# Loading the second half of an expert's weights one job later, behind the transpose of the next rows

## The chip, the core and the metric

The kernel runs on one core of one Trainium2 chip. The metric is the time of one execution on the device in microseconds (us); smaller is better. TensorE (PE in the profile), VectorE (DVE), ScalarE (ACT), GpSimd (POOL) and SyncE (SP) each work through a list of instructions of their own and wait for each other by semaphores. SP computes nothing here: it asks for transfers (DMAs), which 16 DMA engines carry out.

## What is computed

Two stages stand one behind the other. The first is a linear attention with a decaying state, over 4 batches, 8 heads, 768 steps and a head width of 48. Its output, 3072 tokens of 384 numbers, is routed: each token goes to the one expert of 8 with the largest logit.

```python
logits = x @ w_gate + modality_bias[modality_id]
e_idx = np.argmax(logits, axis=1)
...
for e in range(E):
    mask = e_idx == e
    if not mask.any():
        continue
    h = np.maximum(x[mask] @ w1[e], 0.0)          # 384 -> 1024
    out[mask] = gate_w[mask, None] * (h @ w2[e])  # 1024 -> 384
```

Only the experts' part is touched by the change. How many tokens an expert gets is known at run time alone.

## The kernel before

**Jobs.** The tokens of each expert lie side by side in `rows`, in device memory. A job is 128 rows of one expert: they are brought in transposed, multiplied by `w1`, passed through the relu, multiplied by `w2`, scaled and scattered to `out`. Each number is split into a high and a low half-precision part (`whi` and `wlo` for weights, `hh` and `hl` for the hidden layer), so each product is a few matmuls. The first jobs run beside the attention stage. The rest run in the loop at line 1660, whose bounds are read from a table at run time. An expert that is used has at least two jobs in the table; the ends of a run of jobs are marked there.

**One turn of the loop**, job `i`, in the order in which it is written: `finish_up` (the low part of the hidden layer of the job that was begun in the turn before), `take_in` (POOL copies the rows that have arrived, `xn`, to `mxT`, from which TensorE reads, and their gate weights and places, `mn`, to `m2`), `turn` (SP asks for the rows of the job after that: a transpose into `xn` and a small transfer into `mn`), then three branches on a code of the table. If the job is the first of an expert, `go_on` makes the rest of `whi` and `wlo` from the raw weights in `raw`, first `w1` and later, in `blocks(1, ...)`, `w2`. If the next job is the first of another expert, `by_both` takes the sums of squares of that expert's raw weights: ScalarE of the first half of `raw` (`w1`), VectorE of the second half (`w2`, tile `squares`). TensorE's small matmul `pw` (line 982) adds these sums up, and from it come the scales of the next expert's split. Between the branches stand TensorE's matmuls: `low_terms` (L1161), `raise_` (L1082), `high_terms` (L1156).

**The weights.** `raw` holds one expert in single precision, 128 partitions of 6144 numbers, 3 MB, of which `w1` is the first half and `w2` the second. There is one such buffer, so the next expert can be asked for only when the present one has been split. `next_load` does that near the end of the turn. It reads MORE from the table; if that isn't zero, SP issues two transfers of 1536 KB each (L965), one for each half:

```python
def next_load():
    more = self.at(MORE, i, 2 * E - 1, SP)
    with tc.If(more > 0):
        self.load(more % E, 2, 0, 1)
```

**Order.** Each engine runs its instructions in the order written; SP too, and SP's transfers go through one queue. A conditional whose body holds only SP's transfers appears on the other engines as one jump. Where a turn loads nothing, SP adds to the two semaphores that the loads would have added to, so that a wait can count turns; before it adds, it waits until the last load on that semaphore has landed. A reader of `raw` waits for the count that the last load ahead of it in the written order leaves.

Of the kernel before, what the change touches and what calls it, by code (L numbers as in the profile page):

```python
# [25 lines left out]
E = 8  # L26
# [38 lines left out]
ROW, CODE, MORE, SEEN = range(4)  # L65
SP, ACT, AD = (mybir.EngineType.SP,), (mybir.EngineType.Activation,), (mybir.EngineType.Activation, mybir.EngineType.DVE)
# [3 lines left out]
class _Kernel:  # L70
# [1148 lines left out]
    def run(self):  # L1219
# [20 lines left out]
        half = FB * HP // 2  # L1240
# [240 lines left out]
        i, j = NU - 2, NU - 1  # L1481
# [131 lines left out]
        def finish_up():  # L1613
            for g in (1, 2):
                self.relu_low(ph[g], *spans[g])
# [13 lines left out]
        def blocks(m, *at):  # L1629
            for lo, hi in zip(at, at[1:]):  # L1630
                self.broad(m, lo, hi)
                self.rest(m, lo, hi)

        def begin():
            self.broad(0, 0, F0 // 3)

        def go_on():
            self.rest(0, 0, F0 // 3)
            blocks(0, F0 // 3, F0, F0 + F0 // 2, WC)

        def by_both(cols):
            for q in range(NQ):
                if q < NQ // 2:
                    self.norm(junk, q)
                else:
                    part = self.raw[:, q * WQ : (q + 1) * WQ]
                    nc.vector.tensor_tensor_reduce(out=cols, in0=part, in1=part, scale=1.0, scalar=0.0, op0=ALU.mult, op1=ALU.add, accum_out=self.ssq[:, q : q + 1])

        def next_load():
            more = self.at(MORE, i, 2 * E - 1, SP)  # L1650
            with tc.If(more > 0):
                self.load(more % E, 2, 0, 1)

        self.wsb = self.late.tile([P, 1], F32, name="wsb")
        nc.vector.tensor_copy(self.wsb, self.ws[:, 1:])
# [4 lines left out]
        with tc.For_i(1, nj, 1, iteration_sync="reg_based") as i, tc.manual_schedule(engines={getattr(mybir.EngineType, e) for e in MS[:4]}):  # L1660
            finish_up()
            take_in(nc.gpsimd)
            self.turn(0, self.at(ROW, i, E * CAP, SP, 1), mn, xn)
            code = self.at(CODE, i, 15, AD)
            with tc.If(code % 8 > 3) as begun:
                go_on()
            with begun.Else():
                with tc.If(code % 2 > 0):
                    by_both(squares)
            self.low_terms(po)  # L1670
            self.put(po, 0, "b")
            with tc.If(code % 8 > 3):  # L1672
                self.undo()
                blocks(1, 0, F2 // 2, F2)
            self.due(m2, i)
            self.raise_(ph[0], *spans[0])
            self.relu_high(ph[0], *spans[0])
            self.raise_(ph[1], *spans[1])
            scaled = self.scales_("2")
            next(scaled)  # L1680
            with tc.If(code % 8 > 3) as first:
                blocks(1, F2, WC)
                self.relu_low(ph[0], *spans[0])
            with first.Else():
                self.relu_low(ph[0], *spans[0])
                for _ in scaled:
                    pass
                nc.vector.tensor_copy(self.wsb, self.ws[:, 1:])
            next_load()
            self.relu_high(ph[1], *spans[1])  # L1690
            self.raise_(ph[2], *spans[2])
            self.relu_high(ph[2], *spans[2])
            with tc.If(code > 7):
                begin()
            self.high_terms(po)
# [60 lines left out]
```

## Time and profile before

| what | value |
|---|---|
| median of 3 runs | 332.32 us (329.65 to 333.73) |
| the profiled execution's own time | 330.74 us |
| its span in the profile | 329.0 us |
| mean granted TensorE clock in it | 0.99 |
| TensorE busy with matmuls | 316.3 us, 96% of the span |
| turns of the loop that load weights | 1 (two transfers) |

The median is of executions without the profiler; the span is what the profiler saw, from first to last instruction, and the profiled execution's own time is 1.74 us more than that. TensorE's high share of busy time says that it seldom rests, not which of its rests the change can reach. For that the turns of the loop are read one by one.

### The profile page before, as it was taken

How to read it: one execution, taken by the hardware profiler on the slowest of the kernel's cores; microseconds unless marked ns; L12 is line 12 of the kernel's file. 1: busy time of each engine (PE TensorE's matmuls, PEld its weight loads, DVE VectorE, ACT ScalarE, POOL GpSimd, SP SyncE). 2: the span in 40 equal slices, each digit the busy share in tenths (PEclk: the TensorE clock that was granted, in tenths of full speed). 3: DMA queues.
4: the chain of work that ended last, by engine and by line, in shares of the span. 5: the costliest groups of instructions: out<-in, count | busy, mean ns of one | idle time of the engine just before them, and what ended most of it. 6: DMA issues, size and time to landing. Idle time of an engine off the chain costs nothing. (4 is left out here: it accounts for less than half of the span.)

```text
span 329.0 us, 13842 instructions
## 1 busy us (share of the span) xinstructions
PE 316.3 (96%) x5056; PEld 259.2 (79%) x5056; DVE 216.5 (66%) x705; ACT 159.4 (48%) x380; POOL 186.8 (57%) x298
## 2 busy tenths in 40 slices
PE   7999999989999999999999999999999999999983
PEld 3888888889797988879789688876688888887652
DVE  6987789795999899978768841276222223336780
ACT  4667677662367546657834341283222222226731
POOL 8997698954999897656377723234323322222212
PEclk9999999998999999999999999999999999999998
DMA  7869688959949954899978332119822212221100
GB/s 214 251 174 303 188 248 269 185 109 243 339 121 221 283 178 90 180 272 258 202 155 260 114 87 57 35 44 339 122 60 48 48 48 48 60 57 26 48 16 28
DMA packets 50748, 49.59 MB, mean 151 GB/s; under 512 B 35573, under 2 KB 44315, under 8 KB 50448
## 3 DMA queue, kind: packets, MB, share of 16 engines
q1 hardware_dynamic: 46480, 37.93, 48.5%
q0 software_dynamic: 3168, 9.47, 8.3%
q10 hardware_dynamic: 1056, 1.58, 1.4%
q8 instruction: 30, 0.49, 0.7%
q14 instruction: 14, 0.11, 0.1%
HBM read 30.55 MB, written 11.44 MB: 128 GB/s over the span
## 5 line engine op out<-in xcount | busy, mean ns | idle before, releaser
L1082 PEld LDWEIGHTS <-whi 128*128 128x128 f16 x1248 | 71.0, 99 | 4.8 <-issue 2.0
L1156 PEld LDWEIGHTS <-hh 128*128 128x128 f16 x384 | 36.1, 98 | 24.1 <-issue 1.8
L1082 PE MATMUL phb<-mxT,whi 128*128 128x128 f16 x672 | 44.5, 219 | 1.0 <-POOL mxT L1620 0.8
L1091 DVE SCALAR_TENSOR_TENSOR hl<-phb,hh 128x256 f16<-128x256 f32 (+1 forms) x42 | 20.1, 509 | 34.7 <-PE pw L982 17.9
L1082 PEld LDWEIGHTS <-wlo 128*128 128x128 f16 x624 | 37.0, 99 | 0.3 <-DVE wlo L1025 0.3
L380 POOL TENSOR_TENSOR rc<-ud,powr 112x512 f32<-112x512 f32 x23 | 30.4, 1323 | 9.3 <-DMA ud<-in_pd 9.2
L1086 ACT ACTIVATE hh<-phb 128x256 f16<-128x256 f32 (+1 forms) x42 | 18.8, 453 | 30.8 <-PE L1082 12.5
L682 POOL DMA_INDIRECT rows<-row,posi x24 | 26.1, 1089 | 10.7 <-issue 9.1
L1082 PE MATMUL phs<-mxT,whi 128*128 128x128 f16 x480 | 31.1, 223 | 0.9 <-DMA mxT<-rows 0.9
L458 DVE TENSOR_TENSOR at<-psc,mask 128x512 f32<-128x512 f32 x48 | 31.6, 680 | 0.1
L452 PE MATMUL psc<-rc,kc 64*128 64x128 f32 (+1 forms) x384 | 28.6, 285 | 0.8 <-DVE rc L380 0.4
L1161 PEld LDWEIGHTS <-hl 128*128 128x128 f16 x192 | 18.4, 98 | 13.6 <-issue 1.7
L564 ACT ACTIVATE row<-py,sx 128x384 f16<-128x384 f32 x24 | 13.9, 581 | 30.4 <-DVE sx L338 22.5
L452 PEld LDWEIGHTS psc<-rc,kc 64*128 64x128 f32 (+1 forms) x384 | 23.7, 187 | 3.8 <-issue 1.7
L1050 POOL TENSOR_TENSOR seenb<-otb,putb 128x1 int32<-128x1 int32 x13 | 3.8, 295 | 39.7 <-ACTq L1672 31.0
L487 PE MATMUL py<-kv,at 128*64 128x48 f32 x768 | 26.4, 222 | 0.0
L1156 PE MATMUL po<-wlo,hh 128*128 128x384 f16 x112 | 25.2, 326 | 1.1 <-DVE wlo L1025 1.1
L1082 PE MATMUL phb<-mxT,wlo 128*128 128x128 f16 x336 | 25.8, 219 | 0.2 <-DVE wlo L1025 0.2
L487 PEld LDWEIGHTS py<-kv,at 128*64 128x64 f32 x768 | 25.0, 138 | 0.5
L1620 POOL COPY mxT<-xn 128x768 f16<-128x768 f16 x13 | 10.8, 828 | 25.5 <-PE L1156 17.9
L1156 PE MATMUL po<-whi,hh 128*128 128x384 f16 x112 | 25.1, 326 | 0.0
L1039 ACT ACTIVATE otb<-po,fac 128x384 f32<-128x384 f32 x13 | 7.5, 577 | 34.8 <-PE phb L1082 31.6
(317 smaller groups left out, 690.5 us busy)
## 6 DMA issues: line engine op xcount, KB each, us to landing
ud<-in_pd SPq DMA_DIRECT2D x24, 384.0 KB, 4.9
kv<-in_pt SPq DMA_DIRECT2D x24, 384.0 KB, 4.6
raw<-in_w SPq DMA_DIRECT2D x12, 512.0 KB, 4.9
raw<-in_w SPq DMA_DIRECT2D x2, 1536.0 KB, 7.6
r<-in_pt SPq DMA_DIRECT2D x10, 192.0 KB, 6.2
rows<-pad ACTq DMA_DIRECT2D x1, 1544.0 KB, 6.8
rows<-row,posi POOLq DMA_INDIRECT x24, 5.0
xn<-rows SPq DMA_TRANSPOSE x14, 3.0
```

The costliest lines, as they stand in the source:

```text
L380: return (engine or nc.gpsimd).tensor_mul(u["rc"][:R, s], u["rT"][:, s], self.powr[:R, s])
L452: nc.tensor.matmul(u["ps"][j][:, pr * P : (pr + 1) * P], u["kc"][r, pr, :], u["rc"][r, pr, :], start=True, stop=True)
L458: return nc.vector.tensor_mul(u["at"][:, j * NPR : (j + 1) * NPR, :], u["ps"][j].rearrange("p (q t) -> p q t", q=NPR), self.mask.unsqueeze ...
L487: nc.tensor.matmul(py[t, sl], u["at"][:, j * NPR + pr, t], u["v"][:, sl], start=c == h == 0, stop=h == H - 1 and i >= BARE, skip_group_che ...
L564: self.nc.scalar.activation(u["x16"][:, :DM], u["x"], AF.Copy, scale=u["g"]["sx"][:, b : b + 1])
L682: i = nc.gpsimd.indirect_dma_start(out=self.rows, out_offset=bass.IndirectOffsetOnAxis(ap=u["posi"][:, b : b + 1], axis=0), in_=u["row"][: ...
L1082: self.nc.tensor.matmul(ph[:, q * n : (q + 1) * n], w[:, c0 : c0 + P], x[:, xq, :], start=i == q == 0, stop=i == len(terms) - 1, skip_grou ...
L1086: self.nc.scalar.activation(self.hh[:, f0 : f0 + fb, t * P : (t + 1) * P], p3, AF.Relu)
L1091: self.nc.vector.scalar_tensor_tensor(self.hl[:, f0 : f0 + fb, r], p3, 0.0, self.hh[:, f0 : f0 + fb, r], ALU.max, ALU.subtract)
L1156: self.nc.tensor.matmul(po[:, :DM], self.hh[:, f, t * P : (t + 1) * P], w[:, c0 : c0 + DM], start=n == 0, stop=False)
L1161: self.nc.tensor.matmul(po[:, :DM], self.hl[:, f, t * P : (t + 1) * P], self.whi[:, c0 : c0 + DM], start=False, stop=f == FB - 1)
L1620: take_in = lambda e: (e.tensor_copy(self.xT[:, :, :P], xn), e.tensor_copy(m2[:, 0, :], mn[:, 0, :]))
```

## The change

`next_load` gets two arguments: whose entry of the table is read, and which half is loaded. The first half (`w1`) is asked for where both were, near the end of turn `i`. The second half (`w2`) is asked for in turn `i + 1`, by the entry of job `i`, directly behind `turn`, which asks for the next rows. The table is now read twice in a turn by SP, and there are two conditionals in place of one.

```diff
-        def next_load():
-            more = self.at(MORE, i, 2 * E - 1, SP)
+        def next_load(job, half):
+            more = self.at(MORE, job, 2 * E - 1, SP)
             with tc.If(more > 0):
-                self.load(more % E, 2, 0, 1)
+                self.load(more % E, 2, half)
...
             self.turn(0, self.at(ROW, i, E * CAP, SP, 1), mn, xn)
+            next_load(i - 1, 1)
             code = self.at(CODE, i, 15, AD)
...
-            next_load()
+            next_load(i, 0)
             self.relu_high(ph[1], *spans[1])
```

On SP, before, the two halves (`raw`) stand one behind the other under one conditional, behind the transpose (`xn`) and the small transfer (`mn`); the words in brackets are the semaphores that each waits for, and DMAHW2 and DMAHW3 are those of the two loads:

```order
L1068 DMA_TRANSPOSE xn<-rows 128x6x128 [waits DMAHW0_I-4593_own,Pool_I-4593_own,DMAHW2_49]
L1665 UNCONDITIONAL_BRANCH
L1069 ISA
L1069 DMA mn<-rows 128x4 [waits DMAHW1_I-4593_own,Pool_I-4593_own,DMAHW3_49]
L1672 UNCONDITIONAL_BRANCH
L1681 UNCONDITIONAL_BRANCH
L951 ISA
L951 TENSOR_LOAD tab
L1651 COMPARE_AND_BRANCH
L965 ISA
L965 DMA raw<-in_w 128x3072 [waits DVE_I-4593_own,DMAHW2_I-4593_own,Activation_I-4593_own,Activation_49]
```

The next row but one there is the second half, on DMAHW3. After the change the load that comes first in the turn is the second half, and it now has DMAHW2; the first half comes after it, on DMAHW3:

```order
L1069 DMA mn<-rows 128x4 [waits DMAHW1_I-4593_own,Pool_I-4593_own,DMAHW3_49]
L951 ISA
L951 TENSOR_LOAD tab
L1651 COMPARE_AND_BRANCH
L965 ISA
L965 DMA raw<-in_w 128x3072 [waits DVE_I-4593_own,DMAHW2_I-4593_own,Activation_I-4593_own,Activation_49]
L1651 UNCONDITIONAL_BRANCH
L1651 UNCONDITIONAL_BRANCH [waits DMAHW2_I-4593_own]
L1666 UNCONDITIONAL_BRANCH
L951 ISA
L951 TENSOR_LOAD tab
L1651 COMPARE_AND_BRANCH
```

The second half has moved from behind the first half to the front of the following turn, behind `mn`. On VectorE, at the sums of squares of the next expert (`squares`, second half of `raw`), before:

```order
L951 TENSOR_LOAD tab
L1665 REGISTER_ALU
L1665 COMPARE_AND_BRANCH
...
L1668 COMPARE_AND_BRANCH
L1647 REGISTER_ALU
L1647 ISA squares,wssq<-raw 128x1024 [waits DMAHW3_I-4593_own,DVE_I-4593_own]
L1647 ISA wssq 128x1
```

And after:

```order
L1651 UNCONDITIONAL_BRANCH
L951 ISA
L951 TENSOR_LOAD tab
L1666 REGISTER_ALU
L1666 COMPARE_AND_BRANCH
...
L1669 COMPARE_AND_BRANCH
L1647 REGISTER_ALU
L1647 ISA squares,wssq<-raw 128x1024 [waits DMAHW2_I-4593_own,DVE_I-4593_own]
L1647 ISA wssq 128x1
```

VectorE waits for the semaphore of the second half as before. But the last load of it ahead of this instruction is now in the same turn, not in the one before, and there is a jump more (L1651) ahead of the table's read.

## Rows read from the trace of the kernel before

**Rows 1.** The page: span, busy time, and the loads issued inside the loop.

```profile
span 329.0 us, 13842 instructions
PE 316.3 (96%) x5056; PEld 259.2 (79%) x5056; DVE 216.5 (66%) x705; ACT 159.4 (48%) x380; POOL 186.8 (57%) x298
raw<-in_w SPq DMA_DIRECT2D x2, 1536.0 KB, 7.6
```

**Rows 2.** Timeline of PE, 224 to 252: start, duration, engine, line, operation, [idle before].

```profile
226.32 1.46 PE L1161 MATMUL po<-whi,hl 128*128 128x384 f16 x8
...
234.26 1.46 PE L1161 MATMUL po<-whi,hl 128*128 128x384 f16 x8
236.51 1.50 PE L1082 MATMUL phb<-mxT,whi 128*128 128x128 f16 x24 [0.79 <-POOL mxT L1620]
...
243.16 1.46 PE L1161 MATMUL po<-whi,hl 128*128 128x384 f16 x8
244.46 1.50 PE L1082 MATMUL phb<-mxT,whi 128*128 128x128 f16 x24
245.80 0.83 PE L1082 MATMUL phb<-mxT,wlo 128*128 128x128 f16 x12
...
251.10 1.46 PE L1161 MATMUL po<-whi,hl 128*128 128x384 f16 x8
```

**Rows 3.** Timeline of POOL, 223 to 242.

```profile
223.30 0.93 POOL L1620 COPY mxT<-xn 128x768 f16<-128x768 f16 x1
224.49 1.13 POOL L1620 COPY mt<-mn 128x4 int16<-128x4 int16 x1 [0.26 <-DVE ids L1217]
...
235.64 0.82 POOL L1620 COPY mxT<-xn 128x768 f16<-128x768 f16 x1 [4.74 <-PE po L1161]
...
241.31 0.82 POOL L1620 COPY mxT<-xn 128x768 f16<-128x768 f16 x1 [2.76 <-PE L1156]
```

**Rows 4.** Timeline of SP's transfers, 220 to 231 (the first row merges both loads).

```profile
221.44 4.59 SPq L965 DMA_DIRECT2D raw<-in_w  x2
227.46 2.23 SPq L1068 DMA_TRANSPOSE xn<-rows  x1
229.98 0.36 SPq L1069 DMA_DIRECT2D mn<-rows  x1
```

**Rows 5.** Same stretch, all engines: the second of the two loads alone.

```profile
225.70 0.33 SPq L965 DMA_DIRECT2D raw<-in_w  x1
```

**Rows 6.** What SP waited for, 216 to 227: total, times, longest.

```profile
SPq L965 <- DVE wlo L1025: 6.2, 2, 3.6
```

**Rows 7.** Tile raw, from 180 on: its loads, issue to landing.

```profile
DMA to landing us min/median/max: 6.7/7.6/8.5
```

**Rows 8.** Line 1068, the transposes, the whole run: issue to landing.

```profile
DMA to landing us min/median/max: 2.9/3.0/8.0
```

**Rows 9.** What SP waited for in the loop (from 190 on).

```profile
SPq L1068 <- POOL mxT L1620: 43.8, 12, 4.6
```

**Rows 10.** Timeline of all engines in the turn that takes the sums of squares.

```profile
296.92 0.82 POOL L1620 COPY mxT<-xn 128x768 f16<-128x768 f16 x1 [1.89 <-PE L1156]
...
297.81 1.26 SPq L1068 DMA_TRANSPOSE xn<-rows  x1
...
299.36 0.36 SPq L1069 DMA_DIRECT2D mn<-rows  x1
299.48 1.22 DVE L1647 CUSTOM_DVE_ANT_0 squares<-raw 128x1024 f16<-128x1024 f32 x1 [1.08 <-issue]
...
303.39 0.08 DVE L1647 DVE_READ_ACCUMULATOR2_ANT wssq<- 128x1 f32 x1
...
303.62 0.17 PE L982 MATMUL pw<-wssq,onesb 128*128 128x6 bf16 x1 [0.36 <-DVEq L1672]
```

**Rows 11.** Line 1651 on SP, 300.0 to 301.2: the semaphore additions of that turn.

```profile
L1651 SPq EVENT_SEMAPHORE  x2: 17/17/17, 300.5 to 300.6; - x2
```

**Rows 12.** Line 1647 in that turn: VectorE's checks of its semaphores.

```profile
L1647 DVEq EVENT_SEMAPHORE  x3: 21/21/50, 299.3 to 302.1; - x3
```

**Rows 13.** Line 1651, the whole run, all engines (these are all its rows).

```profile
L1651 SPq EVENT_SEMAPHORE  x24: 17/17/17, 211.1 to 308.9; - x24
L1651 SPq COMPARE_BRANCH  x14: 73/118/141, 210.7 to 308.4; - x14
```

## The prediction

> **What bounds the kernel now.** I read the page first: TensorE is busy for 316.3 of 329.0 us [rows 1]. That doesn't yet say where it rests, so I went on to its timeline, turn by turn of the loop. A plain turn lasts from one `low_terms` (L1161) to the next: 243.16 to 251.10, 7.94 us [rows 2]. Inside it nothing is lost: the eight matmuls of L1161 start 1.30 us before the next group, the 24 of the next group 1.34 us before the one after, so about 0.16 us for each 384 columns and 0.056 us for each 128. A turn has 24 of the one and 72 of the other, 24 x 0.1625 + 72 x 0.0558 = 7.92 us. A change can gain only in the turns that are longer than that, and can lose in any.
>
> The load is issued in one turn alone, since the page counts two transfers [rows 1]. The turn that pays for it is 234.26 to 243.16, 8.90 us, with a wait of 0.79 us of TensorE for `mxT`, POOL's copy of the rows [rows 2]. That copy began at 235.64 [rows 3]; in plain turns it begins 1.85 us before L1161 starts (241.31 against 243.16), so it was due at 234.26 - 1.85 = 232.41. The name that the row gives as its releaser is a long finished engine; what came last must be the transpose that fills `xn`. SP's timeline agrees: the transpose was issued at 227.46, behind both loads [rows 4], and one transpose of the run took 8.0 us to land where the median is 3.0 [rows 8]; 227.46 + 8.0 = 235.46, just ahead of the copy.
>
> **The change part by part. The transpose moves ahead of the second half.** SP issued the first half at 221.44, then stood 3.6 us until VectorE had read `raw` to the end [rows 4, 6], issued the second half at 225.70 to 226.03 [rows 5], and came to the transpose 1.43 us later. Now SP goes straight on after the first half: 221.44 + 0.33 + 1.43 = 223.2. There it waits for POOL to have copied the last rows out of `xn`, which ends at 223.30 + 0.93 = 224.23 [rows 3], so the transpose is issued at about 224.3, 3.2 us sooner and behind one half instead of two. It lands after 3.0 us at the least (227.3) and after 8.0 us at the most (232.3) [rows 8]. The copy is due at 232.41, so even the slow one is in time. Gain: the whole excess of the turn, 8.90 - 7.94 = 0.96 us; the lower end is the recorded wait alone, 0.79 us.
>
> **The second half is issued later.** Behind the transpose come `mn`, the read of the table and the branch. With the slow issue of this turn, `mn` starts 2.52 us after the transpose (227.46 to 229.98) and takes 0.36; from the end of `mn` to the end of the branch it is 300.5 - 299.72 = 0.8 us [rows 10, 11]. So it is issued at about 228, and lands 6.7 to 8.5 us later [rows 7], 235 to 236.5. Its data is wanted by the sums of squares at 299.48 [rows 10], over 60 us later. VectorE's last read of the old half, which held the second load at 225.70, is long over. No cost.
>
> What it is now ahead of is the transpose after that, issued when POOL has copied the rows at 232.41 + 0.82, at 233.3, some 5 us behind the half. The copy that needs it is due at 241.31 - 0.96 = 240.35. If it lands after 3.0 us it is early by 4, if after 8.0 us (241.3) late by about 0.95. I take no cost: in the run before the slow transpose came 1.4 us behind a half with another half ahead of that; here there is one half with 5 us to run off. The upper end, 0.95 us, stays for a rival.
>
> **A wait that was not there.** This is the term on the other side. VectorE's `squares` wait for the load of the second half that stands last ahead of them in the program. Before, that was the load step of the turn before, over by then. Now it is the step of the same turn, behind `turn`, also in a turn that loads nothing, where SP only adds to the semaphore. So in the one turn that takes the sums of squares VectorE waits until SP has come past the transpose and `mn`. That is late: POOL's copy holds the transpose until 297.81, `mn` starts at 299.36, and SP's additions are at 300.5 [rows 10, 11], whereas VectorE began at 299.48 [rows 10]. Its last check before it was at 299.3 or a little after [rows 12], so from a check to the start it is some 0.13 us: the start moves to 300.63, by 1.15 us. It may be 0.9 if SP, with three jumps fewer between the transpose and the addition, comes sooner, and 1.25 if the start follows the check by 0.1 us more.
>
> Behind this wait stands `pw`. TensorE was ready for it at 303.62 - 0.36 = 303.26 and was already waiting for VectorE [rows 10], so nothing covers the delay: TensorE loses all of 1.15 us, and what hangs on `pw` (scales, the first piece of the next split) moves with it. ScalarE's sums read the first half, which is asked for at the old place, so they don't wait. The same new wait stands before the split of `w2` in the turns that change experts, but there the split of `w1` comes first, some 4 us of VectorE, and covers it.
>
> **One more branch and table read in each turn.** On SP they lie under its wait for POOL, 43.8 us in 12 turns [rows 9]. On the other four engines a jump is added. In the trace line 1651, which has such a jump on each of them now, has records on SP alone [rows 13], and the plain turn has 7.94 us for 7.92 us of matmuls with five such jumps in it [rows 2]. So I take 0 for TensorE, at most 0.02 / 5 = 0.004 us a turn. VectorE's jump stands between the sums and what `pw` waits for in the one turn that has no cover; the nearest row is the shortest branch of that line on SP, 0.073 us [rows 13], which I add. The Trainium skill (Advanced Engine Details and Errata, Control Flow Timing) gives about 51 ns for a branch that is always taken. By that, 13 turns would cost 13 x 0.051 = 0.66 us, an estimate from that page; the plain turn speaks against it for TensorE, which runs ahead of its matmuls.
>
> **Sum.** -0.96 + 1.15 + 0.07 = +0.26 us: the gain in one turn is given back in another. Against the profiled execution's 330.74 us that is 331.00 (span 329.3). The median of the runs is 332.32, and they lie between 329.65 and 333.73; the four executions have a mean of 331.61, which I take as the level: 331.61 + 0.26 = 331.87, so **331.9 us**. A measurement of this kernel can tell some 2% from no change, 6.6 us; the whole change is about a twenty-fifth of that.
>
> **The rivals.**
> *The new wait doesn't bite* (SP's addition comes sooner, or VectorE's wait is met by an earlier count): only the gain is left, 331.61 - 0.96 = 330.65. For it: at two other readers of the half the wait is covered. Against it: the additions at 300.5 stand in the trace, 1 us behind VectorE's start.
> *The half now lands on the next transpose* (slower): the transpose issued at 233.3 is held by the half issued at about 228, lands 8.0 us later, and TensorE waits 0.95 us one turn after the wait that went. Then nothing is gained: 331.61 + 1.15 + 0.07 = 332.8. It decides itself at a landing of 240.35 - 233.3 = 7.05 us. Against it: 5 us of lead.
> *The change doesn't do what it says*: the transpose is still so late behind the first half that most of the 0.96 stays. That would need more than 8.1 us to land, above the slowest seen. Also 332.8.
> *The jumps cost on every turn*, the 0.073 us of the shortest branch [rows 13] on an engine that TensorE waits for: 13 turns (12 with two additions each, one with loads) x 0.073 = 0.95 on top, 331.87 + 0.95 = 332.8. For it: the loop's chain runs through all engines. Against it: the plain turn is full of matmuls.
>
> **How the numbers follow.** Forecast 0.58, the wait doesn't bite 0.16, the half on the next transpose 0.09, no gain 0.05, the jumps 0.12. The cases lie between 330.65 and 332.8. To these comes the level: single executions go from 329.65 to 333.73, which is more than all of the cases differ, and a median lies in the inner part of that. 330.65 less 0.8 and 332.8 plus 0.7 gives 329.8 to 333.5. No case comes near 2%: within 2% 0.97, faster 0.015, slower 0.015, for a mechanism that none of the rows shows.
>
> **What would show it.** Right: on SP the order first half, transpose, `mn`, second half; the transpose issued near 224.3 and the copy of the rows no later than 1.85 us before L1161; the turn that was 8.90 us long down to 7.9; `squares` starting about 1.1 us later behind L1161 than before and `pw` after a wait of about 1.5 us in place of 0.36; plain turns unchanged at 7.94. Wrong: a turn of 8.9 us one job later, plain turns longer than 7.95, or a `pw` that waits 0.4 us as before.

## The result, and the profile after

The changed kernel takes 332.43 us, the kernel before 329.95 us (medians of 21 runs each). The ratio is 1.0053, with a 95% interval of 1.0030 to 1.0077. So it is slower by 1.75 us (0.0053 x 329.95), at least 1.0 and at most 2.5. The predicted 331.9 us is near the median of the changed kernel, but that is no merit: the level under it was taken too high (331.61 against 329.95), and the difference, +0.26 us, lies below the interval. Four of the traces used further down (*jump only*, *both behind turn*, *changed, fourth* and *both behind sums*) were taken at a lower mean clock, 0.977 to 0.986, so of them the lengths of turns are used and no spans.

The profiled execution took 331.2 us, its span is 329.5 us against 329.0 [rows 1]. It came to the loop 1.41 us earlier than that of before (the first L1161 of the loop starts at 207.58, not 208.99). The comparison is therefore made by turns, from one L1161 to the next.

The page of the changed kernel (the first group is [rows 1] again):

```profile
span 329.5 us, 13911 instructions
PE 316.8 (96%) x5056; PEld 258.0 (78%) x5056; DVE 216.4 (66%) x705; ACT 159.5 (48%) x380; POOL 189.6 (58%) x298
```

The timeline of the changed kernel, SP's transfers and POOL's copies in the turns around the load, answers to [rows 3 to 5]:

```profile
220.81 0.34 SPq L965 DMA_DIRECT2D raw<-in_w  x1
223.66 1.43 SPq L1068 DMA_TRANSPOSE xn<-rows  x1
225.38 0.35 SPq L1069 DMA_DIRECT2D mn<-rows  x1
226.72 0.34 SPq L965 DMA_DIRECT2D raw<-in_w  x1
...
232.48 0.82 POOL L1620 COPY mxT<-xn 128x768 f16<-128x768 f16 x1 [1.76 <-PE po L1156]
```

Here the change does what it says. The transpose stands between the halves, POOL's copy follows it in time, and TensorE's turn behind the load, 8.90 us in [rows 2], is 233.63 to 241.57, 7.94 us. The slowest transpose of the run lands after 5.3 us, not 8.0 [rows 8]:

```profile
DMA to landing us min/median/max: 2.9/3.0/5.3
```

The loss is in the turn that takes the sums of squares, which answers to [rows 10, 11]. Its timeline, all engines:

```profile
296.05 0.82 POOL L1620 COPY mxT<-xn 128x768 f16<-128x768 f16 x1 [2.56 <-PE po L1156]
...
296.94 1.26 SPq L1068 DMA_TRANSPOSE xn<-rows  x1
...
297.22 1.46 PE L1161 MATMUL po<-whi,hl 128*128 128x384 f16 x8
...
298.49 0.36 SPq L1069 DMA_DIRECT2D mn<-rows  x1
...
299.30 1.40 PE L1082 MATMUL phb<-mxT,whi 128*128 128x128 f16 x22 [0.50 <-ACT junk L968]
299.85 1.23 DVE L1647 CUSTOM_DVE_ANT_0 squares<-raw 128x1024 f16<-128x1024 f32 x1 [2.48 <-SPq L1651]
...
301.14 0.84 PE L1082 MATMUL phb<-mxT,wlo 128*128 128x128 f16 x12 [0.44 <-DVE wssq L1647]
...
303.98 0.17 PE L982 MATMUL pw<-wssq,onesb 128*128 128x6 bf16 x1 [0.96 <-DVEq L1673]
```

Line 1651 of that turn, on SP (the first of the two semaphore additions is that of the second half):

```profile
L1651 SPq EVENT_SEMAPHORE  x2: 17/17/17, 299.7 to 300.5; - x2
```

VectorE's `squares` now name SP's line 1651 as what released them, and start 0.15 us behind its addition, 2.63 us behind L1161. Before it was 0.71. The turn lasts 10.39 us instead of 8.47, +1.92 where the prediction had +1.15. Two waits at other places were not foreseen at all, that for ScalarE's `junk` and that for `wssq`. The expert's turn, in which a new expert begins (215.53 to 225.69), grew from 9.38 to 10.16 us. In the loop that makes +0.78 - 0.96 + 1.92 + 0.09 = +1.83 us, with the last 0.09 from the turn behind the sums (10.89 to 10.98). That this is near the measured 1.75 us is chance: as further traces show below, a part of it is no cost of the change.

One more row was out of place in every plain turn. ScalarE's rows of one such turn of the changed kernel, from its timeline:

```profile
275.13 0.58 ACT L1039 ACTIVATE otb<-po,fac 128x384 f32<-128x384 f32 x1 [2.62 <-PE phb L1082]
277.31 0.60 ACT L1086 ACTIVATE hh<-phb 128x512 f16<-128x512 f32 x1 [1.59 <-PE phb L1082]
278.92 0.38 ACT L1086 ACTIVATE hh<-phb 128x256 f16<-128x256 f32 x1 [1.02 <-PE phb L1082]
```

The L1161 of this turn starts at 273.39, so the second `hh` starts 5.53 us behind it. In the trace of before it is 4.79, with a wait of 0.37 us for TensorE. TensorE's own rows are equally dense in both. I call this the lag: what waits for the later results of TensorE in a turn is released some 0.7 us later. It hides in plain turns (7.94 to 7.98 us), where the next user comes later still.

### The profile page after: what moved, and what is told of

The parts are those of the page before. It is cut to its first block, busy times and chain, and to the rows that moved or that the text cites. A ratio compares the mean times of both kernels' runs of the same rounds, so it can differ in the third digit from the quotient of the medians.

```text
span 329.5 us, 13911 instructions
## 1 busy us (share of the span) xinstructions
PE 316.8 (96%) x5056; PEld 258.0 (78%) x5056; DVE 216.4 (66%) x705; ACT 159.5 (48%) x380; POOL 189.6 (58%) x298
## 3 DMA queue, kind: packets, MB, share of 16 engines
q10 hardware_dynamic: 1056, 1.58, 1.4%
## 5 line engine op out<-in xcount | busy, mean ns | idle before, releaser
L1082 PEld LDWEIGHTS <-whi 128*128 128x128 f16 x1248 | 70.0, 98 | 4.1 <-ACT whi L1021 0.8
L1082 PE MATMUL phb<-mxT,whi 128*128 128x128 f16 x672 | 44.9, 219 | 1.0 <-ACT whi L1021 0.5
L1082 PEld LDWEIGHTS <-wlo 128*128 128x128 f16 x624 | 36.4, 98 | 1.1 <-DVE wssq L1647 0.6
L1082 PE MATMUL phs<-mxT,whi 128*128 128x128 f16 x480 | 30.1, 219 | 0.1
L452 PE MATMUL psc<-rc,kc 48*128 48x128 f32 (+1 forms) x384 | 29.1, 289 | 0.5 <-DVE rc L380 0.2
L1161 PEld LDWEIGHTS <-hl 128*128 128x128 f16 x192 | 18.3, 98 | 13.8 <-issue 1.7
L452 PEld LDWEIGHTS psc<-rc,kc 48*128 48x128 f32 (+1 forms) x384 | 24.4, 191 | 3.6 <-DVE rc L380 1.2
L1082 PE MATMUL phb<-mxT,wlo 128*128 128x128 f16 x336 | 25.9, 219 | 0.6 <-DVE wssq L1647 0.4
L387 POOL TENSOR_TENSOR kt<-kv,wtok 128x384 f32<-128x384 f32 x20 | 23.1, 1156 | 0.7 <-ACT wtok L184 0.6
```

Source lines behind the costliest of these rows:

```text
L387: nc.gpsimd.tensor_mul(u["kt"][:, :, R0:], u["k"].rearrange("p (a d) -> p a d", a=NPR), self.wtok)
L452: nc.tensor.matmul(u["ps"][j][:, pr * P : (pr + 1) * P], u["kc"][r, pr, :], u["rc"][r, pr, :], start=True, stop=True)
L1082: self.nc.tensor.matmul(ph[:, q * n : (q + 1) * n], w[:, c0 : c0 + P], x[:, xq, :], start=i == q == 0, stop=i == len(terms) - 1, skip_grou ...
L1161: self.nc.tensor.matmul(po[:, :DM], self.hl[:, f, t * P : (t + 1) * P], self.whi[:, c0 : c0 + DM], start=False, stop=f == FB - 1)
```

## The experiments

Sixteen runs on four chips: A (the first four), B (the next four), C (the third and fourth group), D (the last two).

**Is the lag a matter of the added jumps?** Four kernels on chip A. *Jump only* is the kernel before with

```diff
+        spare = self.late.tile([P, 4], I16, name="spare")
+        def never():
+            more = self.at(MORE, i, 2 * E - 1, SP)
+            with tc.If(more > 2 * E):
+                nc.sync.dma_start(spare, self.rows[bass.ds(more, P), 2 * DM :])
...
             self.turn(0, self.at(ROW, i, E * CAP, SP, 1), mn, xn)
+            never()
```

> The kernel before, with one more conditional of SP alone behind `turn`, which is never taken (its body would fetch a few bytes into a tile that nobody reads). No load is moved. In every turn of the changed kernel ScalarE's second `hh` (of ph1) starts 5.46 us behind the start of L1161 where it was 4.79 before, though TensorE's own rows are as dense as ever; call that the lag. Theory J+ (an additional jump on TensorE early in the turn makes the lag): 5.46 here too, and some 0.8 us in each of the two turns that the lag costs (expert change, sums of squares), +1.5 us, ratio 1.0047. Theory J- (the lag comes from the loss of the jump in the middle of ph2's matmuls, which stays here): 4.79, ratio 1.000 within 0.002. Theory W (the lag comes from the moved transfers and their new waits): 4.79, ratio 1.000 within 0.002.

Measured: ratio 0.9975 (0.9938 to 1.0012). The second `hh` stands 5.43 to 5.53 us behind L1161, the expert's turn is 10.08 us, that of the sums 8.94. The trace agreed with "a jump more makes the lag", the time did not.

*Jump back* is the changed kernel with the same `never` at the old place:

```diff
             next_load(i, 0)
+            never()
             self.relu_high(ph[1], *spans[1])
```

> The changed kernel, with a conditional of SP alone, never taken, behind the load of the first half, at the old place in the source between the relu of ph1 and the matmuls of ph2. The loads stay where the change puts them. TensorE's jumps then stand at 10, 10, 14, 18, and three at 127 in the run of 196 weight loads and matmuls of a turn, none at 153 (the schedule puts the new one with the one of L1682 ahead of it). Theory J- in its narrow form (only a jump inside ph2's group helps): lag as in the changed kernel, second `hh` at 5.46, ratio to the kernel before 1.005. Theory J- in its wide form (any jump behind ph1's matmuls helps): 4.8, ratio 1.0005, since the wait of the squares, 1.15 us, and the gain of 0.96 us remain. Theory J+ (more jumps, more lag): above 5.46, ratio 1.005 or more. Theory W: 5.46, ratio 1.005.

Measured: ratio 1.0044 (1.0010 to 1.0077), `hh` at 5.5, the turns as in the changed kernel (10.15, 7.94, 10.41). No help from a jump there.

*Late half* asks for the second half a job later, but at the old place in the turn (against the changed kernel):

```diff
-            next_load(i - 1, 1)
             code = self.at(CODE, i, 15, AD)
...
+            next_load(i - 1, 1)
             next_load(i, 0)
             self.relu_high(ph[1], *spans[1])
```

> The second half is asked for a job later, as in the change, but not behind `turn`: its conditional stands next to that of the first half, at the old late place. The transpose is still ahead of the second half, TensorE's jumps stand where they stood before (6, 18, 131, and now two at 153), and the squares again wait for a load step of the turn before. Theory J (either form with the place as the cause): second `hh` at 4.79 behind L1161, no wait of the squares; only the gain of 0.96 us is left, ratio 0.997. Theory W (the lag comes from asking for the half a job later): lag 5.46 and 1.5 us lost against the gain of 0.96, ratio 1.0017. J+ by the mere number of jumps: also about 1.0017.

Measured: ratio 0.9977 (0.9939 to 1.0015). No wait of the squares, as expected (1.18 us behind L1161), but the lag is here, with TensorE's jumps where they were. So their place is not its cause.

*Both behind turn* is the kernel before with its one conditional, both halves in it, moved behind `turn`:

```diff
-            more = self.at(MORE, i, 2 * E - 1, SP)
+            more = self.at(MORE, i - 1, 2 * E - 1, SP)
...
             self.turn(0, self.at(ROW, i, E * CAP, SP, 1), mn, xn)
+            next_load()
...
-            next_load()
             self.relu_high(ph[1], *spans[1])
```

> One conditional as in the kernel before, but both halves are asked for in it behind `turn`, a job later. TensorE's jumps: 10, 10, 18, 131, 165, none at 153, one fewer than in the changed kernel. Theory J- (loss of the jump at 153): second `hh` at 5.46, ratio about 1.005 as in the changed kernel or more, since ScalarE's sums now wait for SP too. Theory J+ (one jump too many): 4.79, and only the wait of the sums against the gain, +0.2 to +0.6 us, ratio 1.0005 to 1.002. Theory W (a wait or a transfer behind `turn`): 5.46, ratio 1.005.

Measured: ratio 1.0238 (1.0181 to 1.0296), far more than expected. Now ScalarE waits for SP as well, for the split of the first half and for its sums, and TensorE behind it. Two rows of TensorE's timeline, in the expert's turn and in that of the sums:

```profile
226.53 1.18 PE L1082 MATMUL phb<-mxT,whi 128*128 128x128 f16 x18 [2.29 <-ACT whi L1021]
```

```profile
310.14 1.87 PE L1082 MATMUL phb<-mxT,whi 128*128 128x128 f16 x22 [2.20 <-ACT junk L968]
```

These are the prediction's new wait, at two places where nothing covers it; a third, 1.73 us for `whi`, stands in the next change of experts. The three turns last 12.17, 11.95 and 13.19 us, where *before, third* further down has 10.07, 8.98 and 10.51: 7.75 us more, and the timing gives 7.9 (0.0238 x 330.83). And the lag was here with as many jumps as before. My theory of the jumps fell: all five traces with the lag were of changed loops, but nothing in the loops explained it.

**Is it a matter of the kernel at all?** On chip B both kernels again, unchanged.

> The kernel before once more, unchanged, for a second profile of it. Open from the first four kernels: the lag (ScalarE's second `hh` at 5.4 to 5.5 us behind L1161 instead of 4.79) stands in the traces of all five kernels with a changed loop, however their jumps lie, and in none of before's plain turns; and the turn of 8.90 us, whose 0.96 us the change wins back, is not in the trace of the kernel with a jump alone, whose loads are issued at the same places. Theory L (the lag belongs to the program: before has not got it): 4.79 in every plain turn again. Theory X (the lag belongs to the execution, a program may have it in one and not in another): 5.4 to 5.5 in some turns or all. Theory S (the stall behind the load is a matter of how the transpose happens to land, 6.7 or 8.0 us): the turn after the load's is 7.94 us here or something between; if the stall is a fixed cost of the order of the issues, it is 8.9 again.

> The changed kernel once more, unchanged, for a second profile. Theory L: second `hh` 5.5 us behind L1161 in every plain turn, the squares 2.6 us behind L1161 in their turn, that turn 10.4 us and the expert's turn 10.15. Theory X: 4.79 in some turns or in all, then the squares at about 1.9, their turn 9.6 and the expert's turn 9.4.

Measured: neither has the lag. (Each ran once, 332.53 and 329.87 us, too few for a ratio.) ScalarE in a plain turn of *before, again* (its L1161 starts at 260.83):

```profile
264.65 0.60 ACT L1086 ACTIVATE hh<-phb 128x512 f16<-128x512 f32 x1 [1.50 <-PE L1082]
265.62 0.38 ACT L1086 ACTIVATE hh<-phb 128x256 f16<-128x256 f32 x1 [0.37 <-PE phb L1082]
```

That is 4.79 us. In *changed, again* it is 4.79 too, and its turns are 9.58, 7.95, 9.70 and 10.97. The lag goes with the execution and not with the change.

**The wait by itself.** *Behind sums* is the changed kernel with the conditional moved behind the readers of the half in the program; SP still issues it behind `turn`:

```diff
-            next_load(i - 1, 1)
             code = self.at(CODE, i, 15, AD)
...
                     by_both(squares)
+            next_load(i - 1, 1)
             self.low_terms(po)
```

> The changed kernel with the conditional of the second half moved from in front of the sums of squares to behind them in the program; on SP it stays where it was, behind `turn`. The squares again wait for the load step of the turn before. Theory T3 (the wait for SP in the turn of the sums is the largest cost of the change): the squares start 1.2 us behind L1161 in place of 2.6, their turn lasts 8.9 us in place of 10.4 and the one after 10.5 in place of 11.0, 1.9 us less than the changed kernel; ratio to before 0.997 to 1.000. If the wait is only a cover for another delay (rival: ScalarE's sums and what follows set the end anyway): the turn of the sums stays above 10 us, ratio 1.004.

Measured: ratio 0.9996 (0.9961 to 1.0032); the squares start 0.81 us behind L1161, that turn is 8.57 us, the others 9.50, 7.95 and 10.93.

*Wait only* adds the wait to the kernel before and moves no load:

```diff
+        def never():
+            more = self.at(MORE, i, 2 * E - 1, SP)
+            with tc.If(more > 2 * E):
+                self.load(more % E, 2, 1)
...
             self.turn(0, self.at(ROW, i, E * CAP, SP, 1), mn, xn)
+            never()
```

> The kernel before with a conditional of SP alone behind `turn`, as in the kernel with a jump alone, never taken, but with the load of the second half as its body, so that the squares must wait for SP's additions in the same turn, as in the changed kernel. No load is moved. Theory T3 with the lag: the squares 2.6 us behind L1161, their turn 10.4 us and the next 11.0, +1.9 us against the kernel with the jump alone, ratio to before 1.003 to 1.006. The prediction's working (the wait alone, SP not later than before): the squares 1.9 us behind L1161, +1.15 us. If the wait costs nothing: as with the jump alone, 8.9 us and ratio 0.998.

Measured: ratio 1.0019 (0.9989 to 1.0049). The squares wait for SP (1.51 us; 2.14 in *changed, fifth*, an unchanged run of the changed kernel further down) and the turn is 9.09 us, +0.61 against *before, again*. That is half of what was expected. SP starts `mn` at 296.53, the squares start 0.74 us behind that, where in the changed kernel it is 1.36 (296.21 to 297.57 in *changed, fifth*). A condition that can never hold costs SP no table read and no comparison (its rows have neither at that place), so it adds to the semaphore some 0.7 us sooner behind `mn`. The `never` of *jump only* and of *jump back* is the same: two semaphore additions more on SP, and no read. A row of each, VectorE of *wait only* and of *changed, fifth*:

```profile
297.27 1.23 DVE L1647 CUSTOM_DVE_ANT_0 squares<-raw 128x1024 f16<-128x1024 f32 x1 [1.51 <-SPq L1656]
```

```profile
297.57 1.23 DVE L1647 CUSTOM_DVE_ANT_0 squares<-raw 128x1024 f16<-128x1024 f32 x1 [2.14 <-SPq L1651]
```

The wait follows the moment of SP's addition to within 0.1 us, as the prediction's working had it.

**Both kernels side by side, with the lag.** Chip C, three kernels unchanged from above.

> The kernel before, unchanged, timed against itself and profiled a third time beside the changed kernel on one chip. The two jobs so far ran on two chips, and the lag (ScalarE's second `hh` at 5.5 instead of 4.79 us behind L1161) was in all four traces of the one and in none of the four of the other. Theory C (the lag comes with the chip or the session, whatever the kernel): this trace and that of the changed kernel both have it or both have not. If it is here: the expert's turn 10.1 us instead of 9.4, the turn of the sums 8.9 instead of 8.5, the next 10.5 instead of 10.9. Theory L (only kernels with another jump can have it): never here. Theory S (the stall of the turn behind the load goes with the landing of one transpose): that turn anywhere from 7.94 to 9.2 us; two traces showed 8.90 and 9.15. Ratio 1.000 within 0.003.

> The changed kernel, unchanged, timed and profiled a third time beside the kernel before on one chip. Without the lag in both: the squares 1.94 us behind L1161 and their turn 9.7, the expert's turn 9.6, the turn behind it 7.95, so +0.2 to +0.6 us by the traces, ratio 1.0005 to 1.002. With the lag in both: the squares 2.6 us behind L1161, their turn 10.4 against 8.9, the next 11.0 against 10.5, and +2 us, ratio 1.005 to 1.007. If the ratio is 1.005 without the lag: the traces miss where the time goes.

> The version with the second half's conditional behind the sums of squares once more, on the same chip as the other two. Without the lag: 8.57 us in the turn of the sums, 9.5 in the expert's, 7.95 behind it, 0.7 to 1.0 us less than before by the traces, ratio 0.997 to 0.998. With the lag: 8.9, 10.1 and 7.95, and the gain of the turn behind the load as far as that stall is there in before, ratio 0.997 to 1.000; 2 us less than the changed kernel.

Measured: ratios 0.9968 (0.9931 to 1.0006) for before against itself, 1.0034 (0.9986 to 1.0082) and 0.9978 (0.9934 to 1.0023). The lag is in all three, in before too. ScalarE of *before, third* (its L1161 starts at 260.50):

```profile
264.31 0.60 ACT L1086 ACTIVATE hh<-phb 128x512 f16<-128x512 f32 x1 [1.50 <-PE phb L1082]
265.98 0.38 ACT L1086 ACTIVATE hh<-phb 128x256 f16<-128x256 f32 x1 [1.07 <-PE phb L1082]
```

So the lag is no cost of the change, though the +1.83 us above holds some of it: with it the kernel before has 10.07, 8.98 and 10.51 us in the expert's turn, that of the sums and the next. TensorE's wait for `junk` comes with it too, 0.53 us in *before, third* and none in *changed, again*; the one for `wssq` comes with the change, and is there in each of its traces.

But *before, third* has no stall behind the load (TensorE's wait for `mxT`, 0.79 us in [rows 2]): its turn there is 7.95 us, as in *jump only*, which issues its loads at the same places. TensorE, from that turn:

```profile
236.66 1.46 PE L1161 MATMUL po<-whi,hl 128*128 128x384 f16 x8
237.96 1.50 PE L1082 MATMUL phb<-mxT,whi 128*128 128x128 f16 x24
```

**Is the stall a matter of the lag?** Chip C once more.

> The changed kernel, unchanged, timed and profiled a fourth time. It has been timed on two chips, and both had the lag (ratio 1.0053 and 1.0034); where the lag is absent it has a trace and a single time only. Theory P (without the lag the prediction's sum holds, +0.2 to +0.6 us): ratio 1.000 to 1.002 if this chip has no lag, and 1.004 to 1.007 if it has. Theory N (the loss is the same on every chip): 1.005 with or without the lag.

> The kernel before, unchanged, for the profile that tells whether this chip has the lag, and how long the turn behind the load is. Theory C (the lag comes with the chip or session): second `hh` at 4.79 or at 5.5 us behind L1161, as in the trace of the changed kernel of this job. Theory S: without the lag the turn behind the load is 8.9 to 9.2 us, with it 7.95, since there the transpose behind both halves has landed within 6.9 us, twice, against 8.2 to 8.5 us.

> The kernel before with its one conditional, both halves in it, moved a job later and behind the sums of squares in the program, so that on SP it stands behind `turn`. Neither ScalarE's nor VectorE's sums wait for SP in their own turn, and there is no jump more than before. If the cost of the change is the wait and nothing else: the turn of the sums 8.5 us without the lag and 8.95 with it, the turn behind the load 7.95, so 0 to 1.2 us less than before, ratio 0.996 to 1.000. If two halves behind one another hold the next transpose: a turn of 8.5 to 9 us one job later, ratio 1.000 to 1.002.

Measured: *changed, fourth* 1.0068 (1.0029 to 1.0107), with the lag. *Before, fourth* has the lag and the stall, a turn of 9.06 us, so my expectation that they exclude each other was wrong. POOL and TensorE, from its timeline:

```profile
237.91 0.82 POOL L1620 COPY mxT<-xn 128x768 f16<-128x768 f16 x1 [4.78 <-PE po L1161]
```

```profile
238.78 0.89 PE L1082 MATMUL phb<-mxT,whi 128*128 128x128 f16 x13 [0.95 <-POOL mxT L1620]
```

*Both behind sums* (the edit of *both behind turn*, with `next_load()` behind `by_both` instead) measured 1.0004 (0.9963 to 1.0045), turns of 10.17, 7.94, 8.96 and 10.60: no wait, and two halves behind one another do not hold the next transpose.

**The changed kernel where there is no lag.** Chip D.

> The changed kernel, unchanged, timed and profiled once more, for the case that this chip has no lag; its own profile tells. Theory P (without the lag the prediction's sum holds): second `hh` 4.79 us behind L1161 and a ratio of 1.000 to 1.002, or 5.5 us and 1.004 to 1.007. Theory N (the loss is the same everywhere): 4.79 us and 1.005.

> The version with the second half's conditional behind the sums of squares, beside the changed kernel on one chip. Theory T3 (the wait is what costs): 1.25 us less than the changed kernel where there is no lag, 1.9 us less where there is; ratio to before 0.996 to 1.000 in both.

Measured: 1.0048 (1.0015 to 1.0081) for the changed kernel, 1.0013 (0.9977 to 1.0048) for *behind sums*. No lag in either (`hh` at 4.79), and the changed kernel loses 1.58 us all the same (0.0048 x 328.73). The loss is there with and without the lag. The squares of *behind sums, third* do not wait for SP:

```profile
297.76 1.22 DVE L1647 CUSTOM_DVE_ANT_0 squares<-raw 128x1024 f16<-128x1024 f32 x1 [1.08 <-issue]
```

## Why the prediction went wrong

The lengths of the four turns that differ, in us, from L1161 to L1161; the others are 7.94 to 7.98 in all of these kernels, but for one of 8.06 in *before, third*:

| kernel | lag | expert | behind load | sums | next | sum |
|---|---|---|---|---|---|---|
| before, as predicted from | no | 9.38 | 8.90 | 8.47 | 10.89 | 37.64 |
| before, again (B) | no | 9.41 | 9.15 | 8.48 | 10.90 | 37.94 |
| before, third (C) | yes | 10.07 | 7.95 | 8.98 | 10.51 | 37.51 |
| before, fourth (C) | yes | 10.11 | 9.06 | 8.98 | 10.52 | 38.67 |
| changed, as shown above | yes | 10.16 | 7.94 | 10.39 | 10.98 | 39.47 |
| changed, again (B) | no | 9.58 | 7.95 | 9.70 | 10.97 | 38.20 |
| changed, third (C) | yes | 10.20 | 7.95 | 10.44 | 10.97 | 39.56 |
| changed, fifth (D) | no | 9.58 | 7.94 | 9.72 | 10.97 | 38.21 |
| behind sums (B) | no | 9.50 | 7.95 | 8.57 | 10.93 | 36.95 |
| behind sums, second (C) | yes | 10.19 | 7.94 | 8.97 | 10.55 | 37.65 |
| behind sums, third (D) | no | 9.50 | 7.95 | 8.58 | 10.93 | 36.96 |

Two terms of the sum failed by their size: the gain, which was taken too large, and the price of the new wait, which was taken too small. The mechanisms behind both were there.

**The gain: "the whole excess of the turn, 8.90 - 7.94 = 0.96 us".** It was right for the execution from which it was read. As a cost of the kernel before it was one sample of a landing that scatters. Six traces issue the loads at the old places. From the transpose's issue to POOL's copy it is 8.18 us in the first (227.46 to 235.64) and 8.45, 8.34, 7.37, 6.91 and 6.85 in the others, and the turn is longer by 0.96, 1.21, 1.12, 0.13, 0.01 and 0.01. The copy of the fourth starts 0.56 us behind its L1161 and TensorE's next group is 0.13 late, so it decides itself near 7.25 us, in the middle of the scatter. The mean of the six excesses is 0.57 us. What scatters is the landing of the loads ahead: the second half lands 8.5, 8.8, 8.7, 8.2, 7.6 and 7.7 us after its own issue in the same six, and the copy starts 1.0 to 1.5 us behind that landing each time. In the changed kernel the transpose stands behind the first half alone, lands 0.8 to 1.0 us behind it, and is in time in all five traces. [rows 8] held the warning, a median of 3.0 and one landing of 8.0, and the working took that one for what always comes. The rival "no gain" was there, but with the change to blame (the transpose still late) and with 0.05. That before may not stall at all was not among the cases.

**The wait that was not there: the mechanism and its place were right, 1.15 us was too low.** Without the lag the squares started 1.94 to 1.96 us behind L1161 (foreseen 0.71 + 1.15 = 1.86), SP's addition came 0.83 us behind the end of `mn` (*changed, fifth*: 296.21 + 0.36 to 297.4; foreseen 0.8), and taking the wait away again is worth 38.20 - 36.95 and 38.21 - 36.96, both 1.25 us. With the lag it is 39.56 - 37.65 = 1.91 us. The timed ratios of the same kernels differ alike, by 1.0048 - 1.0013 = 0.0035 (1.15 us of 328.73) and by 1.0034 - 0.9978 = 0.0056 (1.86 us of 331.49), though each ratio is known to some 0.004 only. With the lag POOL's copy starts 1.17 us ahead of L1161 instead of 1.85 (296.05 against 297.22, and [rows 10]), because it waits for TensorE's count too; so the transpose, `mn` and the addition are 0.7 us later, while VectorE without the wait is later by 0.5 (1.21 behind L1161 in *before, third*). The rest is in the next turn, 10.97 against 10.55. The forecast for `pw`, a wait of 1.5 us in place of 0.36, split into two, with and without the lag: 0.44 for `wssq` at L1082, a place that the prediction did not name, and 0.96 at `pw`.

**"One more branch and table read", "covered": 0.07 was too little.** *Behind sums* has the change's jumps and its later split, and no wait. Without the stall's turn it sums to 29.00 us against 28.74 and 28.79 of before, +0.23; with the lag 29.71 against 29.56 and 29.61, +0.12. It lies in the expert's turn and in that of the sums, not in plain turns, which stay at 7.94 to 7.95. Which of the jumps, table reads and waits makes it was not taken apart. The Trainium skill (Advanced Engine Details and Errata, Control Flow Timing) has about 51 ns for a branch that is always taken. With two conditionals more in a turn than before (*jump back*) the plain turns here stayed at 7.94 to 7.95 us, so for TensorE the runs stand against adding such a price turn by turn.

**The sum, with the terms as measured.** Without the lag 1.25 + 0.23 - g, with it 1.91 + 0.12 - g, where g is what the stall of before costs in the timed runs: 1.48 - g and 2.03 - g. The timings gave 1.58 us (0.5 to 2.7) on chip D without the lag, and 1.75, 1.13 and 2.25 us with it. With g at the traces' mean of 0.57 these would be 0.9 and 1.5, inside the intervals; they fit better with a g below that. *Behind sums* says the same: a change with the gain and without the wait should be faster by g less 0.1 to 0.2, and its three ratios, 0.9996, 0.9978 and 1.0013, are no gain that can be told from zero; nor are those of *late half* (0.9977) and *both behind sums* (1.0004), which have the gain without the wait too. With g at the full 0.96 the sum without the lag would be +0.52 us, at the very edge of what was measured. In the result, whose trace has the lag, the wait is the larger miss, 1.91 - 1.15 = 0.76 us, and the gain, with g at 0.57, the smaller, 0.39; without the lag it is the other way round, 0.10 and 0.39.

**Of the signs named in the prediction**, the order on SP, the early copy, the turn of 7.94 and the plain turns (but for one of 7.98) came as written. The transpose was issued 8.13 us behind the L1161 of the expert's turn (223.66 against 215.53), where 224.3 against 216.94 had been 7.36; the expert's turn itself was 0.78 us longer there. The squares came later by 1.92 instead of 1.1 us (2.63 and 0.71 behind L1161).

**What stays open.** Why the second half, issued in the same order, lands after 7.6 us in one execution and after 8.8 in another; whether profiled executions stall more often than timed ones, since g is seen in traces only, so that its share in the loss is worked out and not shown; and what the lag comes from.

## What to carry to other kernels

A stall that ends with a transfer's landing is a sample: take a second and third profile before its whole length is counted as a gain, and work out from which landing time it decides. In a program built like this one, a transfer under a condition leaves a wait also where it is not issued, for every reader that follows it in the program, until the issuing queue has come past it; put the conditional behind those readers, as *behind sums* does, and the wait is gone at the same place on the queue. None of the versions beat the kernel before by more than the measurement can tell.

## What the runs showed of the hardware

With the same program, and at the same granted clock (0.995 in *before, again*, 0.998 in *before, third*), ScalarE was released by TensorE at two different times. On chips B and D the second `hh` of a plain turn waits 0.27 to 0.37 us for TensorE and starts 4.79 us behind L1161 (4.87 in the loop's first turn of five of them), in all six traces. On chips A and C it waits 0.9 to 1.1 us and starts at 5.4 to 5.6 us, in all ten, but for single turns next to the load. TensorE's own rows are equally dense in both, the first `hh` (3.8 to 3.9 us) and `otb` (1.74 us) do not move. It costs some 0.7 us in the expert's turn and 0.5 in that of the sums and gives 0.4 back in the next (10.07, 8.98 and 10.51 against 9.41, 8.48 and 10.90 in before). The semaphore events in the traces show where it sits: TensorE's additions, 30 ns apart at the least, pause twice in each plain turn of the traces with the lag, for 0.5 to 0.7 us from some 3.2 us behind L1161 and for 0.7 us from 3.8 us, while its matmuls go on; without the lag no pause there is longer than 0.25 us. Nothing shows what makes them pause, so a delay between engines read off one profile may be 0.7 us off on another chip.

A transpose behind loads in SP's queue landed when they had landed. Alone it took 3.0 us; behind the two halves it landed 0.8 to 1.3 us after the second half (7.2 to 8.3 us after its issue, in the four traces that have its landing), behind one half 0.8 to 1.3 us after that half (4.7 to 5.3 us).
